# A second PSUM bank for the first MLP's pre-activations, its stores on SP's queue, and a later start for the first block's attention pairs

## The chip, the cores and the metric

The kernel runs on one core of a Trainium2 chip. The core has five engines that matter here: TensorE (PE, matrix products; its weight loads are listed apart as PEld), VectorE (DVE), ScalarE (ACT), GpSimd (POOL) and SyncE (SP, which here only issues DMAs). PE writes its results to PSUM, of which the kernel uses 8 banks of 128 partitions x 512 fp32 values. The metric is device time in microseconds (us); lower is better.

## The reference

Three stages follow each other. Cut to what matters:

```python
# attention: B, H, S, D = 4, 8, 576, 64; causal window of 128
scores = scale * q @ k.T
scores = where((rel >= 0) & (rel < 128), scores - slopes * abs(rel), -1e9)
attn = exp(scores - max) / (sum + 1e-9)
x = (attn @ v) as 2304 tokens x 512
# first MLP, 512 -> 2048 -> 512
h = x @ w_in;  g = where(h > 0, h, exp(min(h, 0)) - 1);  x = g @ w_out
# second MLP, 512 -> 2048 -> 512
h = x @ w_in2; g = maximum(0.01 * h, h);                 out = g @ w_out2
```

## The kernel before

**Precision.** Every MLP product is split in three matmuls (`split_mm`, L244): each fp32 operand is held as a rounded value and a remainder. The weights come raw from HBM and are split on chip, in 16 pieces per layer (`w_a1`, `w_a2`, `w_ts`, `w_add`, `w_hi`, `w_lo`; L161 to L196): for each piece two ACT passes (L169, L174), a shift and two adds on DVE, one more ACT pass (`w<-wraw`), and a subtraction on POOL and on DVE. `w_tick` (L223) does one such step.

**Attention.** It is done in 36 pairs of steps (a block of 256 tokens and two heads each). A pair goes through `scores` (S: matmuls into PSUM banks s0 and s1, minimum on DVE, exponentials on ACT, normalization on POOL), then `transposes` (T: PE, copied out by ACT as `pt`, masked by `selects` on POOL), then `values` (V: matmuls into `av_ps`). V's result is taken out by a cast on ACT (`values_cast`) and a subtraction on DVE (`values_rest`), which write the first MLP's input `x1`.

**Order of the work.** The first 8 pairs run ahead of everything, in a loop over `FIRST` = 16 steps, in an order written by hand (`Ordered.on`); weight pieces 0 to 2 are converted in it, at the places that `EARLY` gives. Then the first MLP runs over `BLK1`, token blocks J of 512, 256, 512, 512 and 512. A block has 16 tasks c, one per weight piece: `mlp1_h` (12 matmuls into `h_ps`; then exp on ACT L516, two DVE passes L517 and L518, a cast on ACT L519, a subtraction L521 on POOL and DVE) and, two tasks later (`Y_LAG`), `mlp1_y` (12 matmuls that accumulate in banks y0 to y3). The remaining pairs of attention are put between the tasks at the places `starts`. In `first_late` (called inside the first task of J = 0) the last values of the first 8 pairs are computed. Then `mlp2` does the second MLP.

**PSUM banks.** `h_ps` always uses bank "h" (but for one task in "y1", and a few of the last block in "s0"), so the next task's matmuls wait until L518 has read the bank. The transposes of a pair's even step use "h" too; those of its odd step use "s1", as one half of the scores does. `av_ps` uses "c".

**Stores.** When a block's y is complete, `ys` copies go to three buffers (tag "eg", shared with the activations `g`), by ACT and DVE in turn, and are stored to DRAM (`x2T`, L546) by ACT's DMA queue.

A scheduler of the framework places ACT, DVE, POOL and SP instructions outside the hand-written part; PE keeps the program's order.

Of the kernel before, what the change touches and what calls it, by code (L numbers as in the profile page):

```python
# [25 lines left out]
NC = DFF // P  # L26
# [4 lines left out]
BLK1 = [(0, 512), (512, 256), (768, 512), (1280, 512), (1792, 512)]  # L31
# [7 lines left out]

EARLY = [(2, "a1", 0), (3, "a2", 0), (3, "ts", 0), (4, "add", 0), (5, "hi", 0), (6, "lo", 0),  # L40
         (6, "a1", 1), (7, "a2", 1), (7, "ts", 1), (8, "add", 1), (9, "hi", 1), (10, "lo", 1),
         (10, "a1", 2), (11, "a2", 2), (11, "ts", 2), (12, "add", 2), (13, "hi", 2), (14, "lo", 2)]
RAW = 2
RAW_SLOTS = [8, 9, 10, 11, 12, 13, 14, 15]
FIRST = 16
# [38 lines left out]
def attention_elu_leaky_kernel(  # L84
# [11 lines left out]
    nc = tc.nc  # L96
# [34 lines left out]
    x2T = dram.tile([P, NK, NT], F32, name="x2T")  # L131
# [10 lines left out]
    at = {"load": 0, "a": 0, "b": 0, "c": 0}  # L142
# [29 lines left out]
    def w_a2(k):  # L172
        low = raws[k][:, :, :, 0]
        tc.keep_in_program_order(nc.scalar.activation(low, low.bitcast(U32), AF.Copy, scale=2.0 ** -29))  # L174
# [23 lines left out]
    def w_first(k):  # L198
        w_a1(k)
        w_a2(k)  # L200

    def w_second(k):
        w_ts(k)
        w_add(k)

    def w_third(k):
        w_hi(k)
        w_lo(k)
# [14 lines left out]
    def w_tick(last):  # L223

        while at["load"] < min(last, max(at["c"] + STAGED[at["load"] >= NC], W1_EARLY)):
            w_load()
        a, b, c = at["a"], at["b"], at["c"]
        if a < min(last, at["load"]) and a <= b + 1:
            w_first(a)
            at["a"] += 1  # L230
        if b < a:
            w_second(b)
            at["b"] += 1
        if c < b:
            w_third(c)
            at["c"] += 1
# [134 lines left out]
    def scores(k):  # L371

        if 2 * k >= NS:
            return
        ps = score_mm(2 * k)
        score_mm(2 * k + 1, ps, BLK)
        for s in (2 * k, 2 * k + 1):
            score_min(s)
            score_exp(s)
            score_rec(s)  # L380
            score_norm(s)
# [7 lines left out]
    def transposes(s, tag):  # L389

        if s >= NS:
            return
        st = steps[s]
        t = st["t"]
        ps = psp.tile([P, 512], F32, tag=tag, name="pt_ps")
        pt = ptp.tile([P, 512], F32, tag="pt", name="pt")
        st["pt"], st["parts"] = pt, []
        blocks = []
        for t0, n, before, hh, c in st["reg"]:
            if before == P:  # L400
                blocks.append((P, n, c.start, [(t0, n, hh, t0 - P, P), (t0, n, hh, t0, n)]))
            else:
                if before:
                    blocks.append((before, n, c.start, [(t0, n, hh, t0 - before, before)]))
                blocks.append((n, n, c.start + before, [(t0, n, hh, t0, n)]))
        blocks.sort(key=lambda x: (-x[0], -len(x[3])))
        if 0 < s < FIRST:
            warm(ps[:, :BLK], WARM[1])
        col, groups = 0, {}
        for nk, n, c, parts in blocks:  # L410
            tc.keep_in_program_order(nc.tensor.transpose(ps[:nk, col:col + n], t[:n, c:c + nk], ident[:n, :n]))  # L411
            groups.setdefault((nk, len(parts)), []).append((slice(col, col + n), parts))
            col += n
        for (nk, m), g in groups.items():
            c = slice(g[0][0].start, g[-1][0].stop)

            tc.keep_in_program_order(nc.scalar.copy(pt[:nk, c], ps[:nk, c]))  # L417
        st["groups"], st["col"] = groups, col
# [55 lines left out]
    def values_cast(s):  # L474
        if s < NS and steps[s]["out"]:
            xh, _, av = steps[s]["out"]
            act.copy(xh, av)

    def values_rest(s):
        if s < NS and steps[s]["out"]:  # L480
            xh, xl, av = steps[s]["out"]
            dve.tensor_tensor(xl, av, xh.bitcast(F32), op=ALU.subtract)


    def mlp1_h(J, cs, late_work=lambda: None):

        n = BLK1[J][1]  # L490
        xh, xl = X1[J]

        last = J == len(BLK1) - 1
        tag = "s0" if last and cs[0] < LAG2 and (LAG2 - cs[0]) % 2 else "h"
        if J == 0 and cs[0] == 1:
            tag = "y1"
        ps = psp.tile([P, len(cs), n], F32, tag=tag, name="h_ps")
        ws = [weights(1, c, 0) for c in cs]

        late = NK - 1 if cs[0] == 0 else NK  # L500
        order = [(ci, kk) for ci in range(len(cs)) for kk in range(late)]
        order += [(ci, kk) for ci in range(len(cs)) for kk in range(late, NK)]
        for ci, kk in order:
            wih, wil = ws[ci]
            s = slice(kk * P, (kk + 1) * P)
            if (ci, kk) == (0, late):
                late_work()

            split_mm(ps[:, ci, :], wih[:, s], wil[:, s], xh[:, kk, :n], xl[:, kk, :n],
                     ci == 0 and kk == 0, kk == NK - 1, skip_group_check=True)  # L510

        g, hi, lo = (pool.tile([P, 2 * BLK], dt, tag=t, name=t)
                     for pool, t, dt in ((egp, "eg", F32), (glp, "gh", F32R), (glp, "gl", F32R)))
        ps = ps.rearrange("p c n -> p (c n)")
        m = len(cs) * n
        nc.scalar.activation(g[:, :m], ps, AF.Exp)  # L516
        nc.vector.tensor_scalar(g[:, :m], g[:, :m], 1.0, -1.0, op0=ALU.min, op1=ALU.add)  # L517
        nc.vector.tensor_tensor(g[:, :m], ps, g[:, :m], op=ALU.max)  # L518
        nc.scalar.copy(hi[:, :m], g[:, :m])  # L519
        for half, eng in ((slice(0, m // 2), nc.gpsimd), (slice(m // 2, m), nc.vector)):  # L520
            eng.tensor_tensor(lo[:, half], g[:, half], hi[:, half].bitcast(F32), op=ALU.subtract)  # L521
        return hi, lo
# [3 lines left out]
    def mlp1_y(J, cs, gg):  # L526
        gh, gl = gg
        t0, n = BLK1[J]
        per = 512 // n
        if cs[0] == 0:  # L530
            Y[J] = [psp.tile([P, per, n], F32, tag=f"y{i}", name=f"y{i}") for i in range(NK // per)]
        for ci, i, m in [(ci, i, m) for ci in range(len(cs)) for i in range(3) for m in range(NK)]:
            woh, wol = weights(1, cs[ci], 1)
            w, g = ((woh, gh), (woh, gl), (wol, gh))[i]

            matmul(Y[J][m // per][:, m % per, :], w[:, m * P:(m + 1) * P], g[:, ci * n:ci * n + n],
                             start=cs[ci] == 0 and i == 0 and m % per == 0, stop=cs[ci] == NC - 1 and i == 2,
                             skip_group_check=True)
        if cs[-1] == NC - 1:
            for i, y in enumerate(Y.pop(J)):  # L540
                ys = egp.tile([P, per, n], F32, tag="eg", name="ys")
                if i % 2:
                    nc.vector.tensor_copy(ys, y)
                else:
                    nc.scalar.copy(ys, y)
                nc.scalar.dma_start(out=x2T[:, i * per:i * per + per, t0:t0 + n], in_=ys)  # L546


    for x in LOADS:
# [57 lines left out]
        w_early(n)  # L607
    score_rec(FIRST + 1)
    score_norm(FIRST + 1)
    Ordered.on = False  # L610
    at["a"] = at["b"] = at["c"] = 1 + EARLY[-1][-1]
    w_tick(NC)

    pend, done = [], FIRST // 2

    def first_late():
        values_to(FIRST - 1)
        scores(done + 1)  # L620

    for J in range(len(BLK1) - 1):
        t0, n = BLK1[J + 1]
        todo = NPAIR * (t0 + n) // BLK - done
        starts = [i * NC // todo + (NC // todo - 2) // 2 for i in range(todo)]
        for c in range(NC):
            if c in starts:
                head = done == FIRST // 2

                transposes(2 * done + 1, "c" if head else "s1")  # L630
                values_to(2 * done - 1)
                transposes(2 * done, "y0" if head else "h")
                for i in (1, 0):
                    selects(2 * done + i)
                if not head:
                    scores(done + 1)
                done += 1
            elif c == 0 and J:
                values_to(2 * done - 1)
            g = mlp1_h(J, [c], first_late if c == 0 and J == 0 else lambda: None)  # L640
            if len(pend) == Y_LAG:
                mlp1_y(*pend.pop(0))
            if at["c"] < NC:
                w_tick(NC)
            pend.append((J, [c], g))
# [90 lines left out]
    J = len(BLK1) - 1  # L736
# [9 lines left out]
    for x in pend:  # L746
        mlp1_y(*x)
# [50 lines left out]
```

## Time and profile before

| | |
|---|---|
| median of 3 runs | 963.45 us (961.48 to 963.78) |
| the profiled execution | 965.38 us, of which 963.4 us are the span of the profile |
| PE busy | 935.9 us, 97% of the span |
| DVE, ACT, POOL busy | 411.2, 406.5, 236.0 us (43%, 42%, 24%) |
| mean granted clock of PE | 0.989 |
| chain that ended last | 83% PE; DVE 3%, ACT 2% |

PE is the engine that ends last nearly everywhere. A matmul counts as busy for as long as it takes, at a lowered clock too, so the busy time alone doesn't show what PE loses.

### The profile page before, as it was taken

How to read it: one execution, taken by the hardware profiler on the slowest of the kernel's cores; microseconds unless marked ns; L12 is line 12 of the kernel's file. 1: busy time of each engine (PE TensorE's matmuls, PEld its weight loads, DVE VectorE, ACT ScalarE, POOL GpSimd, SP SyncE). 2: the span in 40 equal slices, each digit the busy share in tenths (PEclk: the TensorE clock that was granted, in tenths of full speed). 3: DMA queues.
4: the chain of work that ended last, by engine and by line, in shares of the span. 5: the costliest groups of instructions: out<-in, count | busy, mean ns of one | idle time of the engine just before them, and what ended most of it. 6: DMA issues, size and time to landing. Idle time of an engine off the chain costs nothing.

```text
span 963.4 us, 13126 instructions
## 1 busy us (share of the span) xinstructions
PE 935.9 (97%) x4885; PEld 755.9 (78%) x4885; DVE 411.2 (43%) x1003; ACT 406.5 (42%) x918; POOL 236.0 (24%) x393
## 2 busy tenths in 40 slices
PE   8888999989999999999999999999999999999998
PEld 4566778788777777777878888888888888888886
DVE  5788883455444443444357666421211121111111
ACT  6887763344434343333256666432322232222222
POOL 4864542333343332334123333100000000000000
PEclk9999999899999999999999999999999999999999
DMA  8940420221211011110333335110110010001001
GB/s 279 363 159 23 153 66 22 88 67 53 58 45 45 21 42 64 45 31 1 110 131 133 131 131 179 40 66 1 36 51 1 1 44 1 0 1 44 1 1 44
DMA packets 41758, 66.76 MB, mean 69 GB/s; under 512 B 3680, under 2 KB 27232, under 8 KB 41696
## 3 DMA queue, kind: packets, MB, share of 16 engines
q1 hardware_dynamic: 38704, 61.09, 19.0%
q10 hardware_dynamic: 2992, 4.85, 1.4%
q8 instruction: 38, 0.62, 0.3%
q14 instruction: 24, 0.20, 0.1%
HBM read 56.49 MB, written 9.44 MB: 68 GB/s over the span
## 4 chain that ended last, share of the span: by engine, by line
PE 83%; DVE 3%; ACT 2%; issue 0%; DMA 0%; ACTq 0%; DVEq 0%
PE h_ps L119 38%; PE o_y L119 18%; PE y L119 17%; PE av_ps L119 4%; PE s_ps L119 3%; PE pt_ps L411 2%; PE o_s L119 1%; PE o_c L119 1%; ACT t L110 1%; DVE t L110 1%; DVE eg L518 0%; DVE eg L517 0%; ACT wf L169 0%; ACT wraw L174 0%; DVE stat L110 0%
## 5 line engine op out<-in xcount | busy, mean ns | idle before, releaser
L119 PE MATMUL h_ps<-x,w 128*128 128x512 f32 (+1 forms) x1920 | 429.3, 373 | 10.8 <-DVE eg L518 8.1
L119 PEld LDWEIGHTS h_ps<-x,w 128*128 128x128 f32 x1920 | 337.0, 190 | 83.4 <-DVE eg L518 12.1
L680 DVE TENSOR_TENSOR g2l<-g,g2h 128x512 fp32r<-128x512 f32 (+1 forms) x80 | 52.1, 653 | 269.1 <-ACT g2h L679 269.1
L119 PE MATMUL y<-gh,w 128*128 128x512 f32 (+1 forms) x640 | 159.1, 371 | 2.1 <-DVE eg L518 1.9
L119 PE MATMUL o_y<-w,g2h 128*128 128x512 f32 x512 | 157.7, 389 | 0.0
L675 ACT ACTIVATE g<-h_ps 128x512 f32<-128x512 f32 (+1 forms) x80 | 44.2, 552 | 252.1 <-PE h_ps L119 250.8
L119 PEld LDWEIGHTS y<-gh,w 128*128 128x128 f32 x640 | 114.8, 190 | 23.2 <-DVE eg L518 2.3
L119 PEld LDWEIGHTS o_y<-w,g2h 128*128 128x128 f32 x512 | 96.1, 188 | 20.0
L521 POOL TENSOR_TENSOR gl<-eg,gh 128x256 fp32r<-128x256 f32 (+1 forms) x80 | 71.2, 890 | 161.2 <-ACT gh L519 154.5
L119 PE MATMUL o_y<-w,g2l 128*128 128x512 f32 x256 | 99.6, 389 | 0.0
L110 POOL TENSOR_SCALAR t<-t,stat 128x128 f32<-128x128 f32 (+3 forms) x160 | 63.0, 407 | 90.6 <-DVE stat L110 83.7
L519 ACT CAST gh<-eg 128x512 fp32r<-128x512 f32 (+1 forms) x80 | 46.2, 577 | 89.4 <-DVE eg L518 89.3
L516 ACT ACTIVATE eg<-h_ps 128x512 f32<-128x512 f32 (+1 forms) x80 | 43.9, 551 | 90.7 <-PE h_ps L119 87.8
L110 ACT ACTIVATE t<-t,stat 128x128 f32<-128x128 f32 (+3 forms) x160 | 62.6, 393 | 46.0 <-DVE t L110 32.7
L517 DVE TENSOR_SCALAR eg<-eg 128x512 f32<-128x512 f32 (+1 forms) x80 | 45.5, 569 | 83.3 <-ACT eg L516 81.7
L119 PE MATMUL y<-gl,w 128*128 128x512 f32 (+1 forms) x320 | 79.9, 372 | 0.0
L110 POOL TENSOR_TENSOR w<-wraw,w 128x512 fp32r<-128x512 f32 x32 | 52.7, 1647 | 84.7 <-ACT w L110 84.2
L119 PEld LDWEIGHTS y<-gl,w 128*128 128x128 f32 x320 | 57.9, 192 | 10.2
L110 DVE CUSTOM_DVE_ANT_0 t<-s_ps,bias 128x256 f32<-128x256 f32 (+4 forms) x160 | 51.9, 371 | 16.3 <-PE s_ps L119 15.7
L521 DVE TENSOR_TENSOR gl<-eg,gh 128x256 fp32r<-128x256 f32 (+1 forms) x80 | 42.1, 527 | 38.9 <-ACT gh L519 38.7
L110 POOL TENSOR_SCALAR_AFFINE_SELECT pt<-pt 128x256 f32<-128x256 f32 (+1 forms) x112 | 48.5, 438 | 39.1 <-ACT pt L417 35.2
L119 PEld LDWEIGHTS o_y<-w,g2l 128*128 128x128 f32 x256 | 48.1, 188 | 10.0
(60 smaller groups left out, 788.8 us busy)
## 6 DMA issues: line engine op xcount, KB each, us to landing
wraw<-in_w_in SPq DMA_DIRECT2D x32, 512.0 KB, 3.8
wraw<-in_w_out SPq DMA_DIRECT2D x32, 512.0 KB, 4.7
qkr<-in_kT SPq DMA_DIRECT2D x28, 192.0 KB, 2.9
x2T<-ys ACTq DMA_DIRECT2D x18, 256.0 KB, 2.4
xr<-x2T SPq DMA_DIRECT2D x4, 1024.0 KB, 5.4
qkr<-in_qT SPq DMA_DIRECT2D x28, 128.0 KB, 2.8
out<-os SPq DMA_DIRECT2D x14, 256.0 KB, 2.0
vr<-in_vp SPq DMA_DIRECT2D x16, 192.0 KB, 2.5
```

Of the source, the lines that this page charges most:

```text
L110: ins = f(*args, **kw)
L119: tc.keep_in_program_order(nc.tensor.matmul(*args, **kw))
L411: tc.keep_in_program_order(nc.tensor.transpose(ps[:nk, col:col + n], t[:n, c:c + nk], ident[:n, :n]))
L516: nc.scalar.activation(g[:, :m], ps, AF.Exp)
L517: nc.vector.tensor_scalar(g[:, :m], g[:, :m], 1.0, -1.0, op0=ALU.min, op1=ALU.add)
L519: nc.scalar.copy(hi[:, :m], g[:, :m])
L521: eng.tensor_tensor(lo[:, half], g[:, half], hi[:, half].bitcast(F32), op=ALU.subtract)
L675: nc.scalar.activation(g, ps, AF.Prelu, alpha=0.01)
L680: nc.vector.tensor_tensor(lo, g, hi.bitcast(F32), op=ALU.subtract)
```

## The change

Three things change. (1) In all blocks but the last, `h_ps` alternates between banks "h" and "c": in block 0 the odd tasks use "c", in the others the even ones. "c" is shared with `av_ps`; the use of "y1" goes. (2) The stores of blocks 0 to 2 are issued by SP instead of ACT. (3) In block 0 the pairs start at tasks 3, 7, 11, 15 instead of 1, 5, 9, 13; the scores of pair 9, which stood in `first_late`, move to task 3; weight piece 3 is begun in the hand-written part, and from then on `w_tick` begins piece k + 1 while it ends piece k.

```diff
-         (10, "a1", 2), (11, "a2", 2), (11, "ts", 2), (12, "add", 2), (13, "hi", 2), (14, "lo", 2)]
+         (10, "a1", 2), (11, "a2", 2), (11, "ts", 2), (12, "add", 2), (13, "hi", 2), (14, "lo", 2),
+         (15, "a1", 3)]
...
-        if J == 0 and cs[0] == 1:
-            tag = "y1"
+        if not last and cs[0] % 2 == (J == 0):
+            tag = "c"
...
-                nc.scalar.dma_start(out=x2T[:, i * per:i * per + per, t0:t0 + n], in_=ys)
+                q = nc.sync if J < len(BLK1) - 2 else nc.scalar
+                q.dma_start(out=x2T[:, i * per:i * per + per, t0:t0 + n], in_=ys)
...
-    Ordered.on = False
-    at["a"] = at["b"] = at["c"] = 1 + EARLY[-1][-1]
-    w_tick(NC)
...
     def first_late():
         values_to(FIRST - 1)
-        scores(done + 1)
+        values_cast(FIRST - 1)
+        values_rest(FIRST - 1)
+        w_a2(3)
+        Ordered.on = False
+        at["a"], at["b"], at["c"] = 4, 3, 3
...
-        starts = [i * NC // todo + (NC // todo - 2) // 2 for i in range(todo)]
+        starts = [i * NC // todo + (3 if J == 0 else 0) for i in range(todo)]
...
-                head = done == FIRST // 2
-                transposes(2 * done + 1, "c" if head else "s1")
+                transposes(2 * done + 1, "s1")
                 values_to(2 * done - 1)
-                transposes(2 * done, "y0" if head else "h")
+                transposes(2 * done, "h")
                 for i in (1, 0):
                     selects(2 * done + i)
-                if not head:
-                    scores(done + 1)
+                scores(done + 1)
```

How this moves the instructions is seen at two places. The first is ACT's queue at the start of block 0. `COPY pt<-pt_ps` are the copies of the transposes of pair 8, `eg<-h_ps` is the exponential of a task, `gh<-eg` its cast, and `wf<-wraw`, `wraw<-wraw` and `w_4` are the passes over weight pieces. Before:

```order
L519 CAST gh<-eg 128x512
L169 ACTIVATE wf<-wraw 128x1024
L174 ACTIVATE wraw<-wraw 128x1024
L417 COPY pt<-pt_ps 128x256
L417 COPY pt<-pt_ps 64x256
L417 COPY pt<-pt_ps 128x128
L417 COPY pt<-pt_ps 64x128
L516 ACTIVATE eg<-h_ps 128x512 x2
L110 CAST w_4_917<-wraw 128x2x512
L519 CAST gh<-eg 128x512
```

With the change:

```order
L518 ACTIVATE eg<-h_ps 128x512 x2
L111 CAST w_4_864<-wraw 128x2x512
L521 CAST gh<-eg 128x512
L170 ACTIVATE wf<-wraw 128x1024
L175 ACTIVATE wraw<-wraw 128x1024
L521 CAST gh<-eg 128x512
L170 ACTIVATE wf<-wraw 128x1024
L175 ACTIVATE wraw<-wraw 128x1024
L418 COPY pt<-pt_ps 128x256
L418 COPY pt<-pt_ps 64x256
L418 COPY pt<-pt_ps 128x128
L418 COPY pt<-pt_ps 64x128
```

The four copies stood after the first passes over piece 4; now they stand behind the exponentials of tasks 1 and 2, the end of piece 4 and the first passes over pieces 5 and 6.

The second place is the end of block 0, when its four `ys` are copied and stored. ACT's queue before, with the stores `x2T<-ys`, the cast of V's result (`x_1820`) and the copies of the transposes of the pair at task 2 of block 1:

```order
L545 COPY ys<-y_896 128x512
L545 COPY ys<-y_898 128x512
L546 DMA x2T<-ys 128x512 x3
L110 CAST x_1820<-av_ps 128x256
L546 DMA x2T<-ys 128x512
L417 COPY pt<-pt_ps 128x256 x2
```

ACT's queue there with the change:

```order
L547 COPY ys<-y_843 128x512
L547 COPY ys<-y_845 128x512
L418 COPY pt<-pt_ps 128x256
L111 CAST x_1820<-av_ps 128x256
L418 COPY pt<-pt_ps 128x256
```

And SP's queue with the change, between the loads of queries, keys (`qkr`) and values (`vr`):

```order
L277 DMA qkr<-in_qT 128x256
L278 DMA qkr<-in_kT 128x384
L550 DMA x2T<-ys 128x512 x3
L293 DMA vr<-in_vp 128x3x128
L550 DMA x2T<-ys 128x512
L277 DMA qkr<-in_qT 128x256
```

The four stores have left ACT's queue, so that the first copy of a transpose stands ahead of V's cast and behind no store; on SP they stand between loads, the fourth behind one more load of values.

## Rows read from the trace of the kernel before

**Rows 1.** Busy time by stage: us, PE, PEld, DVE, ACT, POOL, granted clock, DMA share, GB/s.

```profile
47.50:80.20 32.70, 27.63 (x126) 20.89 (x125) 27.75 (x49) 26.29 (x48) 19.53 (x26) 0.95 0.36 125
```

**Rows 2.** Waits over the span: waiter, released by, us in total, times, longest.

```profile
PE h_ps L119 <- DVE eg L518: 8.1, 8, 2.3
PE s_ps L119 <- ACT pt L417: 3.1, 2, 1.9
PEld h_ps L119 <- DVE eg L518: 12.1, 15, 2.8
```

**Rows 3.** Timeline of PE at block 0's start: start, us, what, idle before it.

```profile
49.80 0.66 PE L119 MATMUL av_ps<-pt,qkvr 128*64 128x128 f32 x8
...
62.45 1.44 PE L119 MATMUL y<-gh,w 128*128 128x512 f32 x3 [1.94 <-DVE eg L518]
...
74.65 3.02 PE L119 MATMUL h_ps<-x,w 128*128 128x512 f32 x12 [2.35 <-DVE eg L518]
...
80.23 0.60 PE L411 MATMUL pt_ps<-ident,t 128*128 128x128 f32 x4
```

**Rows 4.** PE in stretches of 2 us: us, busy, granted clock, DMA share, GB/s.

```profile
64.00:66.00 2.00, 2.00 (x6) 0.50 0.00 0
...
174.00:176.00 2.00, 2.00 (x9) 0.50 0.21 59
```

**Rows 5.** Timeline of ACT at the start of block 0.

```profile
48.70 1.11 ACT L169 ACTIVATE wf<-wraw 128x1024 f32<-128x1024 f32 x1
...
66.49 1.15 ACT L169 ACTIVATE wf<-wraw 128x1024 f32<-128x1024 f32 x1
67.53 1.14 ACT L174 ACTIVATE wraw<-wraw 128x1024 int32<-128x1024 uint32 x1
68.56 1.12 ACT L110 CAST w<-wraw 128x1024 fp32r<-128x1024 f32 x1
69.69 0.60 ACT L516 ACTIVATE eg<-h_ps 128x512 f32<-128x512 f32 x1
```

**Rows 6.** Timeline of PE in block 1: where a pair's transposes begin.

```profile
167.99 0.38 PE L411 MATMUL pt_ps<-ident,t 128*128 128x128 f32 x2
...
182.16 0.38 PE L411 MATMUL pt_ps<-ident,t 128*128 128x128 f32 x2
...
228.76 0.38 PE L411 MATMUL pt_ps<-ident,t 128*128 128x128 f32 x2
...
237.29 0.38 PE L411 MATMUL pt_ps<-ident,t 128*128 128x128 f32 x2
```

**Rows 7.** Timeline of DVE, then of ACT with its DMA queue, at block 0's end.

```profile
170.86 0.69 DVE L543 COPY ys<-y 128x512 f32<-128x512 f32 x1 [2.37 <-DMA x2T<-ys]
...
171.59 0.33 ACTq L546 DMA_DIRECT2D x2T<-ys  x1
171.95 0.65 ACT L417 COPY pt<-pt_ps 128x256 f32<-128x256 f32 x2 [1.85 <-DVE x L110]
```

**Rows 8.** Timeline of PE at block 3's start: where transposes begin.

```profile
364.27 0.38 PE L411 MATMUL pt_ps<-ident,t 128*128 128x128 f32 x2
...
382.56 0.38 PE L411 MATMUL pt_ps<-ident,t 128*128 128x128 f32 x2
...
397.49 0.38 PE L411 MATMUL pt_ps<-ident,t 128*128 128x128 f32 x2
```

**Rows 9.** Waits of PE between 190 and 250 us (block 1).

```profile
PE h_ps L119 <- DVE eg L518: 4.3, 5, 0.9
```

**Rows 10.** Timeline of DVE and PE: V's subtraction and the next h.

```profile
112.06 0.42 DVE L110 TENSOR_TENSOR x<-av_ps,x 128x256 fp32r<-128x256 f32 x1
...
111.78 3.02 PE L119 MATMUL h_ps<-x,w 128*128 128x512 f32 x12
...
211.92 0.42 DVE L110 TENSOR_TENSOR x<-av_ps,x 128x256 fp32r<-128x256 f32 x1 [1.04 <-ACT x L110]
...
212.52 1.69 PE L119 MATMUL h_ps<-x,w 128*128 128x256 f32 x12
```

## Prediction

> **What bounds the kernel now.** The chain that ended last is 83% PE, so I looked for the places where PE is held up, first by stage, then by releaser, then in PE's own timeline. In the first 32.7 us of block 0 PE is busy for 27.63 us, while DVE is busy for 27.75 and ACT for 26.29 [rows 1]: this stretch is shared between three engines. Over the whole span PE's matmuls wait 8.1 us for DVE's reading of `h_ps`, and 3.1 us, in two waits, for ACT's copy of transposes, where scores need bank "s1"; weight loads of `h_ps` wait 15 times on the same reading of the bank as matmuls do 8 times [rows 2]. After some of the waits the granted clock is 0.50, the 1.2 GHz level: at 64 to 66 us, behind the wait of 1.94 us, and at 174 to 176 us [rows 3, 4]. So a wait there costs more than its own length, and I price such places by the period of the timeline that holds them.
>
> **Stores by SP (blocks 0 and 2).** At the end of block 0 the fourth `ys` copy on DVE waits 2.37 us for the first store, whose buffer it takes; ACT's queue holds the fourth store until that copy is done, at 171.59; and the transposes' copies stand behind it, with 1.85 us of idle time ahead of them [rows 7]. PE's scores wait for these copies. The pair at 167.99 lasts until the next one at 182.16: 14.17 us. A pair of the same block with no wait, 228.76 to 237.29, lasts 8.53 us [rows 6]. The loss is 5.6 us: the longer wait of the two (1.9 us) [rows 2] and the low clock behind it. In the changed order ACT's first transposes' copy stands behind no store, and V's cast neither. The four stores aren't removed: SP issues them, between loads. It is free there for the first three, and the fourth stands behind a load of values that waits for PE. DVE's fourth copy still waits for the first store and may delay the minimum of the scores by some tenths, but PE needs those only at the next pair. I take the full 5.6 us; at worst, if the minimum's delay goes through, 4.
>
> At the start of block 3 the same chain is there: 364.27 to 382.56 is 18.29 us, the next period, 382.56 to 397.49, is 14.93 [rows 8]. The difference, 3.4 us, goes with it. Block 1 has two stores and no such wait; I count nothing.
>
> A rule speaks against this part. The Trainium skill, DMA: Bandwidth & Descriptors, section "Issuing engines are not separate DMA queues", says that all issuing engines' transfers end up on the same 16 DMA engines and that spreading the issue saves only the sequencer's time, usually small. By that alone the move would be worth the issue times, 0.33 us for the fourth [rows 7], on an engine off the path: about nothing. The trace shows another thing than transfer speed, an instruction queue that is held by a store waiting for another engine; I go by that, and keep the rule's outcome as a rival.
>
> **Two banks for h, block 1.** Between 190 and 250 us PE waits five times for the bank, 4.3 us in all, 0.8 to 0.9 each [rows 9]. It is always the odd task, whose matmuls follow after a single short `y`, while DVE still does the pair's scores before L517 and L518. With the even task in "c", the odd task's bank was emptied by the transposes' copy long before. 4.3 us go. What could take their place is the transposes' own need of normalized scores: all periods fall to about 8.53 us [rows 6], a period that is there already and shows no such need. So the full 4.3; at worst 3.
>
> **Two banks elsewhere.** Weight loads wait 15 times and matmuls 8 times, so some seven tasks lose only a little, a few tenths each where the load is late and the matmul not. I take 0.17 each, 1.2 us in all (between 0 and 2).
>
> **The price of "c".** In 27 pairs (3 in block 0, 24 in blocks 1 to 3) the task after a pair now needs "c" emptied by V's cast and subtraction. Before, it needed the copy of the even transposes. In block 1 the subtraction starts at 211.92 and ends 0.42 later, at 212.34; h starts at 212.52 [rows 10], after the scores. So 0.18 us are left, and it costs nothing while nothing delays DVE. In block 0, where DVE also converts weights, one subtraction runs from 112.06 to 112.48 while h started at 111.78 [rows 10]: there 0.7 us would be lost. Of the three pairs of block 0 I count one such; the small bank waits in block 0 that go (0.2 to 0.4 us each) pay for it.
>
> **The start of block 0.** This is the unclear part. Until the pair at 80.23, PE loses there: 1.94 us and 2.35 us of waits [rows 3] and about half of the 3.5 us at the 1.2 GHz level [rows 4], some 6 us. What the change removes: the scores of pair 9 and the transposes of pair 8 leave the first tasks, so DVE has less ahead of L518, and tasks 1 and 2 no longer wait for one bank. What it adds: at task 3 the transposes go to "s1" and the scores need "s1" again, so PE waits for ACT's copy, which now stands behind two passes over each of pieces 5 and 6. From the ACT rows one pass takes 1.0 us (66.49 to 67.53 to 68.56) and a cast of a piece 1.1 (68.56 to 69.69), an exponential or `gh` about 0.5 [rows 5]. From the first pass of piece 3 at 48.70 [rows 5] up to the copies ACT has eight passes (pieces 3 to 6), two casts of pieces, three exponentials, three `gh` (one per task 0 to 2) and a cast of V: 8.2 + 2.2 + 3.0 + 0.3 = 13.7 us, and four waits for DVE or PE of 0.5 to 0.9 us each, estimated from the chain (each cast of a piece waits for an add on DVE that waits for the pass ahead of it), 2.5 in all. The copies come at about 65. PE meanwhile, from the values at 49.80 to 50.46 on [rows 3], has the last three matmuls of task 0 (0.7 us), three dozens (tasks 1 and 2 and one `y`) of at most 3.0 us each [rows 10] and transposes of 0.6 [rows 3]: it is done at about 61. A wait of some 4 us, with a stretch of low clock behind it, 2 us more: 6 us again. So I take 0 for the start. If ACT's own work alone decided, with no waits in between, the copies would come at 62.5, the wait would be 1.5 us and the gain about 4; if the clock stays low through task 3 and beyond, the loss is about 4.
>
> **Sum.** 5.6 + 3.4 + 4.3 + 1.2 = 14.5 us, the rest zero. The profiled execution took 965.38 us (span 963.4), so its counterpart would take 950.9. The median of the runs, 963.45, is 1.9 below that execution; against it the sum gives 949.0.
>
> **Rivals.** (a) The start of block 0 gains 4 us, since the wait for the copies is short: 945. (b) It loses 4 us, for the wait is long and the clock low: 953. For both speaks that my walk rests on waits that no row shows. (c) "c" binds a little: V's cast and subtraction come 0.3 us later than the scores end in 27 pairs, 8 us: 957. For it speaks the margin of only 0.18 us; against it that the cast stands in ACT's queue right where it stood. (d) The stores by SP bring nothing but issue time, as the rule has it: the 9.0 us stay, 958. Against it speaks that what waits is ACT's queue, for a copy, and not a transfer [rows 7]. (e) The other side: DVE is late for V's subtraction by 0.7 us in every pair, as in the one pair at 112.06 [rows 10], since L517 and L518 of the odd task now come earlier and stand ahead of it: 27 x 0.7 = 18.9, 968. From (14.5 + 2.9) / 27 = 0.64 us per pair on the change is slower; at 0.54 us it makes no difference, 963.5. Against it speaks that DVE is idle for 1.04 us before the subtraction in block 1 [rows 10]. (f) The banks in turn don't remove block 1's wait, for the transposes then wait for normalized scores: the 4.3 us stay, 953.
>
> **Numbers.** 0.3% (2.9 us) is about what a measurement of this kernel can tell from no change. The forecast, 946 to 952, gets 0.60; (a) 0.10, (b) 0.11, (c) 0.07, (d) 0.03, (f) 0.03, (e) 0.03 slower and 0.03 about equal. Faster is all but (e): 0.94, and 0.03 each for the others. The range leaves out the (e) cases, half of (c) and (d) and a part of (a): 943 to 957.
>
> **What would show it.** After: no wait of scores for ACT's copies at the ends of blocks 0 and 2, and no granted clock of 0.5 there; in block 1 no wait of h for L518 and periods of 8.5 us; one wait of scores for ACT's copy at task 3 of block 0, of about 4 us. I am wrong if h waits for V's subtraction in many pairs, if the periods of block 1 don't fall, or if block 0 as a whole moves by more than 4 us.

## The result and the profile after

| | before | with the change |
|---|---|---|
| median | 962.47 us (961.47 to 963.78, 4 runs) | 950.93 us (950.91 to 951.09, 4 runs) |
| ratio | | 0.9879 [0.9865, 0.9893] |
| the profiled execution | 965.38 us, span 963.4 | 951.09 us, span 949.3 |
| its mean granted clock of PE | 0.989 | 0.995 |

The change gains 11.5 us between the medians; forecast were 949.0 us and a range of 943 to 957. The forecast took its 14.5 us from 963.45; from the 962.47 of this table they lead to 948.0. The profiled execution of before, from which the prediction read its prices, lies 2.9 us above the median. Of 42 other runs of that kernel, taken beside the experiments, only two took as long, and their mean granted clocks are 0.991 to 0.996.

The page of the changed kernel, busy time and chain:

```profile
PE 928.4 (98%) x4885; PEld 752.4 (79%) x4885; DVE 409.1 (43%) x1003; ACT 407.0 (43%) x918; POOL 234.1 (25%) x393
...
PE 85%; ACT 1%; DVE 1%; issue 0%; DVEq 0%; ACTq 0%
```

PE's waits over the span (waiter, released by, total, times, longest), against [rows 2]:

```profile
PE s_ps L120 <- ACT pt L418: 4.3, 1, 4.3
...
PE h_ps L120 <- DVE x L111: 1.5, 3, 0.6
...
PE h_ps L120 <- DVE eg L520: 1.3, 1, 1.3
```

Eight waits of h for its bank were 8.1 us; one is left (1.3 us, in the last block of the first MLP, which keeps its bank; it was there before too). The two waits of scores at the ends of blocks 0 and 2 are gone, and a new one of 4.3 us is there. Of the three short waits of h for V's subtraction (`x`) two stand in block 0, at 96.90 and 124.07 us (0.39 and 0.55): that is what bank "c" costs there. The third is at the last pair of all (442.71).

PE's timeline: the start of block 0, then the ends of pairs in blocks 1 and 3, against [rows 3, 6, 8]:

```profile
65.50 2.05 PE L120 MATMUL s_ps<-qkr 64*64 64x192 f32 x10 [4.34 <-ACT pt L418]
67.48 5.43 PE L120 MATMUL h_ps<-x,w 128*128 128x512 f32 x12
...
168.76 0.38 PE L412 MATMUL pt_ps<-ident,t 128*128 128x128 f32 x2
...
177.44 0.38 PE L412 MATMUL pt_ps<-ident,t 128*128 128x128 f32 x2
...
219.52 0.38 PE L412 MATMUL pt_ps<-ident,t 128*128 128x128 f32 x2
...
227.96 0.38 PE L412 MATMUL pt_ps<-ident,t 128*128 128x128 f32 x2
...
353.00 0.38 PE L412 MATMUL pt_ps<-ident,t 128*128 128x128 f32 x2
...
367.90 0.38 PE L412 MATMUL pt_ps<-ident,t 128*128 128x128 f32 x2
```

The pair at the end of block 0 takes 8.68 us (168.76 to 177.44) instead of 14.17, a later one in block 1 8.44, and a pair of block 3 14.90. At task 3 of block 0 the h behind the wait takes 5.43 us, where one at full clock takes 2.9. The clock there (stretch, PE busy, granted clock, DMA share, GB/s):

```profile
62.00:64.00 2.00, 0.00 (x0) 0.62 0.00 0
64.00:66.00 2.00, 0.51 (x4) 0.50 0.00 0
...
72.00:74.00 2.00, 2.00 (x9) 0.82 0.00 0
```

It is at its lower level, 1.2 GHz, to about 72 us. ACT's timeline shows the two passes over a weight piece that stood ahead of the transposes' copies:

```profile
62.74 1.12 ACT L170 ACTIVATE wf<-wraw 128x1024 f32<-128x1024 f32 x1
63.77 1.17 ACT L175 ACTIVATE wraw<-wraw 128x1024 int32<-128x1024 uint32 x1
64.84 0.91 ACT L418 COPY pt<-pt_ps 128x256 f32<-128x256 f32 x4
```

**Where the time went.** The stages of the profiled executions, measured in PE's timeline between the first h, the first transposes of blocks 1, 2 and 3, and the end, in us (the last four columns are kernels of the next section; one execution each):

| | before | change | e1_banks | e2_stores | e6_nopairs | e3_pairs |
|---|---|---|---|---|---|---|
| ahead of block 0 | 47.52 | 46.82 | 47.03 | 46.61 | 47.85 | 47.19 |
| block 0 | 107.67 | 109.14 | 107.14 | 107.13 | 108.46 | 106.42 |
| its end and block 1 | 82.10 | 72.00 | 76.20 | 76.93 | 71.99 | 79.06 |
| block 2 | 112.51 | 110.56 | 110.93 | 112.16 | 110.54 | 112.52 |
| from block 3 on | 613.60 | 610.78 | 612.60 | 610.57 | 611.66 | 611.71 |

10.1 of the 14.1 us between the two profiled executions come from the end of block 0 and block 1, 2.0 from block 2, 2.8 from the rest and 0.7 from ahead of block 0; block 0 itself is 1.5 longer. Block 0 is the same in before, e1, e2, e6 and e7 (108.43 there), and took 107.1 to 108.5 us in their executions, so that the 109.14 of the change are only 0.7 above the longest of these.

### The profile page after: what moved, and what is told of

Its sections match the earlier page's. It is cut to its first block, busy times and chain, and to the rows that moved or that the text cites. A ratio compares the mean times of both kernels' runs of the same rounds, so it can differ in the third digit from the quotient of the medians.

```text
span 949.3 us, 13158 instructions
## 1 busy us (share of the span) xinstructions
PE 928.4 (98%) x4885; PEld 752.4 (79%) x4885; DVE 409.1 (43%) x1003; ACT 407.0 (43%) x918; POOL 234.1 (25%) x393
## 4 chain that ended last, share of the span: by engine, by line
PE 85%; ACT 1%; DVE 1%; issue 0%; DVEq 0%; ACTq 0%
PE h_ps L120 39%; PE o_y L120 18%; PE y L120 18%; PE av_ps L120 4%; PE s_ps L120 3%; PE pt_ps L412 2%; PE o_s L120 1%; PE o_c L120 1%; ACT wf L170 0%; ACT wraw L175 0%; DVE wraw L111 0%; DVE eg L519 0%; DVE w L111 0%; DVE eg L520 0%; ACT w L111 0%
## 5 line engine op out<-in xcount | busy, mean ns | idle before, releaser
L523 POOL TENSOR_TENSOR gl<-eg,gh 128x256 fp32r<-128x256 f32 (+1 forms) x80 | 69.8, 872 | 151.2 <-ACT gh L521 139.8
L523 DVE TENSOR_TENSOR gl<-eg,gh 128x256 fp32r<-128x256 f32 (+1 forms) x80 | 42.1, 526 | 39.4 <-ACT gh L521 39.0
L111 DVE CUSTOM_DVE_ANT_0 t<-s_ps,bias 128x256 f32<-128x256 f32 (+4 forms) x160 | 52.0, 371 | 13.4 <-PE s_ps L120 13.2
L120 PEld LDWEIGHTS o_y<-w,g2l 128*128 128x128 f32 x256 | 48.0, 188 | 10.1
```

The costliest lines, as they stand in the source:

```text
L111: ins = f(*args, **kw)
L120: tc.keep_in_program_order(nc.tensor.matmul(*args, **kw))
```

## The experiments

All kernels compute the whole reference; e5_warm adds work. The first four ran on one chip, against 963.44 us of before there (11 runs); e3, e4, e5 and e8 on one against 963.69 (17 runs); e9, e10 and e11 against 961.52 (7); e12 against 962.70 (7). So ratios are what is compared across these groups.

**e1_banks: the banks of blocks 1 to 3 alone, on the kernel before.**

```diff
+        if J and not last and cs[0] % 2 == 0:
+            tag = "c"
```

> The kernel before with one edit: in blocks 1 to 3 the even tasks put h_ps into bank c; block 0, the stores and the pairs stay. My theory (the odd task of block 1 only waits for its one bank): the five waits of 0.8 to 0.9 us in block 1 go, and some tenths at four tasks of block 2, together about 6 us: 956.5 us. The two stalls behind the stores stay. Rival (the pair's own chain of scores, normalization and transposes sets the pace of block 1): the wait turns up ahead of the transposes, and the time stays within 1.5 us of before, 962.

956.40 us, ratio 0.9929 [0.9916, 0.9943]: 7.0 us, as expected. Between 190 and 250 us PE has no wait left. The two waits of scores are still there.

**e2_stores: the stores by SP alone, on the kernel before.**

```diff
-                nc.scalar.dma_start(out=x2T[...], in_=ys)
+                q = nc.sync if J < len(BLK1) - 2 else nc.scalar
+                q.dma_start(out=x2T[...], in_=ys)
```

> The kernel before with one edit: the stores of blocks 0 to 2 go to SP's queue. My theory (ACT's queue is held by the fourth store, which waits for the fourth copy): both stalls behind the stores go, 5.6 and 3.4 us: 953.5 us. Rival (only the issue time is saved, as for a move between queues that share the same DMA engines): 962, unchanged.

957.22 us, 0.9937 [0.9924, 0.9951]: 6.2 us. No wait of scores for ACT's copies is left, as the mechanism wants, but the gain is smaller than the 9.0 of the prediction. PE's timeline at the end of block 0 there:

```profile
166.54 0.38 PE L411 MATMUL pt_ps<-ident,t 128*128 128x128 f32 x2
...
168.29 1.13 PE L119 MATMUL s_ps<-qkr 64*128 64x256 f32 x8
...
175.53 0.38 PE L411 MATMUL pt_ps<-ident,t 128*128 128x128 f32 x2
```

The scores run through, and the pair takes 8.99 us.

**e7_late4: all stores stay on ACT; only the fourth one of blocks 0 and 2 is issued after the next pair.**

```diff
-                nc.scalar.dma_start(out=x2T[...], in_=ys)
+                st = lambda i=i, ys=ys: nc.scalar.dma_start(out=x2T[...], in_=ys)
+                if J in (0, 2) and i == 3:
+                    late_store.append(st)
+                else:
+                    st()
...
                     scores(done + 1)
+                while late_store:
+                    late_store.pop()()
```

> The kernel before with one edit: the stores stay on ACT's queue, but the fourth one of blocks 0 and 2 is issued behind the next pair's transposes and scores. My theory (what counts is that the store stands ahead of the transposes' copies in ACT's queue, not which queue it is on): nearly the same gain as by SP, 8 to 9 us less what issuing costs on ACT: 954 us. Rival (the gain comes from SP's queue itself, as a second queue): at most 2 us, 961.

958.54 us, 0.9949 [0.9935, 0.9964]: 4.9 us, most of what SP's queue brings, without SP; the 954 of the expectation rested on the price of 9.0 that e2 had not borne out either. ACT's queue and PE's scores at the end of block 0 there:

```profile
170.68 0.37 ACT L417 COPY pt<-pt_ps 128x256 f32<-128x256 f32 x1 [1.12 <-PE av_ps L119]
...
172.50 0.33 ACTq L546 DMA_DIRECT2D x2T<-ys  x1
170.66 1.57 PE L119 MATMUL s_ps<-qkr 64*128 64x256 f32 x8
```

The copies run ahead of the fourth store, and the scores run through. So it is the place of the fourth store in ACT's queue that cost the time. From issue to landing the stores take as long by either queue (us in the last place; before, then the change):

```profile
x2T<-ys ACTq DMA_DIRECT2D x18, 256.0 KB, 2.4
x2T<-ys SPq DMA_DIRECT2D x10, 256.0 KB, 2.6
```

The Trainium skill, DMA: Bandwidth & Descriptors, section "Issuing engines are not separate DMA queues", says that transfers issued by different engines run on the same 16 DMA engines, and that issuing from several saves only the issue time. The landing times agree with the first; by the second alone e2 would have given 962.

**e6_nopairs: banks of blocks 1 to 3 and stores; block 0 as before.**

```diff
+        if J and not last and cs[0] % 2 == 0:
+            tag = "c"
...
-                nc.scalar.dma_start(out=x2T[...], in_=ys)
+                q = nc.sync if J < len(BLK1) - 2 else nc.scalar
+                q.dma_start(out=x2T[...], in_=ys)
```

> The change without its third part: banks in turn in blocks 1 to 3 and the stores by SP, block 0 as before. My theory (the later start of the pairs brings nothing at block 0's start and costs 1.5 us there, 113.5 against 112.0 us): both gains add up, 15 us: 947.5 us, some 1.5 to 3 us faster than the whole change. Rival (the pairs' later start is part of the gain): 953 or more.

950.90 us, 0.9873 [0.9858, 0.9888]: the same as the whole change. The 947.5 of my theory, with 1.5 to 3 us won back at block 0, did not come. The two parts add up (7.0 + 6.2 = 13.2, together 12.5), and the third, with block 0's banks, is worth nothing that these runs can tell beside them. It isn't needed for them either.

**e3_pairs: the later pairs alone (the change, with h's banks and the stores as before).**

```diff
-        if not last and cs[0] % 2 == (J == 0):
-            tag = "c"
+        if J == 0 and cs[0] == 1:
+            tag = "y1"
...
-                q = nc.sync if J < len(BLK1) - 2 else nc.scalar
-                q.dma_start(out=x2T[...], in_=ys)
+                nc.scalar.dma_start(out=x2T[...], in_=ys)
```

> The change's third part alone (later pairs in the first block; h on bank h but for the second task, stores by ACT, as before). My theory: it neither gives nor takes at the start of block 0, so 963.5 against 963.4 of before, up to 2.5 more if the odd tasks of block 0 without a bank of their own wait again; a wait of scores for ACT's copies of some 4 us stands at task 3 and the two waits at the ends of blocks 0 and 2 (about 1.2 to 1.9 each) are back. Rival, that the later pairs are what the other two parts need in order to gain, or that they carry some of the 12.5 us: then 960 or less alone, or over 966.

959.84 us, 0.9976 [0.9957, 0.9994], with the widest spread of all (958.4 to 966.3 in 12 runs). It gains 0.6 to 4.1 us alone (the interval), where I had expected none; the median is that of the rival (960 or less), of which e6 excludes the first half: the other two parts gain without it. Nor was the wait of 4 us at task 3 there. PE stood still earlier, where `y` needs bank "y1", which the second task's h still held. Its profile has the wait at the end of block 0 too, and shows why the stores' price is hard to read from one execution:

```profile
60.06 1.46 PE L120 MATMUL y<-gh,w 128*128 128x512 f32 x3 [2.56 <-DVE eg L519]
...
65.97 1.18 PE L120 MATMUL s_ps<-qkr 64*64 64x192 f32 x10 [0.26 <-ACT pt L418]
...
166.41 0.38 PE L412 MATMUL pt_ps<-ident,t 128*128 128x128 f32 x2
...
170.52 1.13 PE L120 MATMUL s_ps<-qkr 64*128 64x256 f32 x6 [1.66 <-ACT pt L418]
...
177.53 0.38 PE L412 MATMUL pt_ps<-ident,t 128*128 128x128 f32 x2
```

The wait is 1.66 us and the pair 11.12, against 14.17 in the profiled execution of before, whose wait was 1.9; behind the wait of e3 the granted clock is 1.00, there it was 0.50 for three stretches and 0.80 for one. Between the two profiled executions, of before and of e3, 4.6 of 6.5 us lie in this pair (3.05) and in the first one of block 3 (1.6), behind waits that the stores by SP remove anyway. That may be why e3's gain is nothing beside the other parts; one execution each doesn't show it.

**e4_defer: the change, with pair 9's scores behind task 3's h and y.**

```diff
-                scores(done + 1)
+                if J or c != 3:
+                    scores(done + 1)
...
                 mlp1_y(*pend.pop(0))
+            if J == 0 and c == 3:
+                scores(done)
```

> The change, with the scores of pair 9 behind task 3's h and y in block 0 instead of ahead of them, so that PE has 6 us of work while ACT comes to the transposes' copies. My theory: the wait of 4.3 us and the low clock behind it (3.9 us lost) are what the start of block 0 still costs; both go, 951 - 8 = 943, or 945 if a little of the wait stays. Rival, the three engines share this stretch, so that the stall comes back at the next bank (task 4's h, or the exponentials of the deferred scores): 949 to 951.

952.99 us, 0.9886 [0.9871, 0.9902], the ratio of the change (0.9879); the 8 us of my theory did not come. The wait at task 3 is gone, and PE comes to the second pair (task 7) at 85.77 instead of 91.83; there it stands still:

```profile
91.88 0.68 PE L412 MATMUL pt_ps<-ident,t 64*128 64x64 f32 x4 [2.93 <-DVE eg L520]
...
95.07 2.05 PE L120 MATMUL s_ps<-qkr 64*64 64x192 f32 x10 [1.68 <-ACT pt L418]
```

The rival was right in kind: the stall moves on, with its low clock (0.50 from 90 to 100 us), most of it to the second pair, and only 0.90 us to a task's bank ahead of that.

**e8_tick: the change, with the weight step of task 2 behind the pair at task 3.**

```diff
                 done += 1
+                if J == 0 and c == 3:
+                    w_tick(NC)
...
-            if at["c"] < NC:
+            if at["c"] < NC and (J or c != 2):
```

> The change, with the weight step of task 2 of block 0 moved behind the pair at task 3, so that two of ACT's passes over a weight piece (2.1 us) stand behind the transposes' copies instead of ahead. My theory, by which ACT's queue sets the wait: it falls from 4.3 to about 2.2 us, 949, or 947 if the low clock is shorter too. Rival, the wait is set by something else than ACT's passes (DVE's adds, or the copies' own inputs), so it stays at 4 and the time at 951; or the later weight piece delays task 5's y, 951 to 953.

952.74 us, 0.9884 [0.9867, 0.9900], again the ratio of the change, where 949 was expected. The wait at task 3 falls as ACT's queue wants, to 2.26; the rest returns at the second pair:

```profile
63.75 1.18 PE L120 MATMUL s_ps<-qkr 64*64 64x192 f32 x10 [2.26 <-ACT pt L418]
...
90.64 0.45 PE L412 MATMUL pt_ps<-ident,t 64*128 64x64 f32 x4 [0.71 <-DVE eg L520]
...
93.87 2.05 PE L120 MATMUL s_ps<-qkr 64*64 64x192 f32 x10 [2.32 <-ACT pt L418]
```

**e5_warm: the change, with 36 matmuls on the identity into the scores' own bank ahead of pair 9's scores.** They are extra work, and the scores overwrite them.

```diff
-        ps = score_mm(2 * k)
+        ps = None
+        if k == FIRST // 2 + 1:
+            ps = [psp.tile([P, 512], F32, tag=tg, name="s_ps") for tg in ("s0", "s1")]
+            warm(ps[0][:, :BLK], 36)
+        ps = score_mm(2 * k, ps)
```

> The change with 36 extra matmuls (128 x 256, on the identity, bf16) into the scores' own bank s0 ahead of pair 9's scores, which overwrite it: added work that falls into the wait for ACT's copies. My theory: the low clock behind the wait comes of PE standing still there; the copies come no later, so that the wait is filled and the clock stays at 1.0: 951 - 3.9 + about 0.5 for what the extra matmuls reach beyond the wait = 947.5. Rival, the low clock there doesn't hang on PE standing still (it is at 0.62 already at 62 to 64): 951 or, with the added work on the path, up to 954.

951.08 us, 0.9867 [0.9852, 0.9882]: nothing gained that is clear of noise. The clock did stay up where the wait was filled, and fell at the second pair, behind waits of 0.19 and 0.66 us there:

```profile
64.00:66.00 2.00, 2.00 (x20) 1.00 0.00 0
...
96.00:98.00 2.00, 2.00 (x6) 0.58 1.07 346
```

Three ways to shorten the start thus came to the same second pair, where V's subtraction on DVE started at 96.50 (e4), 95.25 (e8), 95.45 (e5) and 96.43 (change). Counted from each execution's first h, that is at most 2.3 us earlier than in the change, where wait and low clock at task 3 were 8. So DVE and ACT, more than PE, set the time of block 0 up to there. The change's DVE and POOL in one task of that stretch:

```profile
86.07 1.83 POOL L111 TENSOR_TENSOR w<-wraw,w 128x512 fp32r<-128x512 f32 x1 [3.15 <-ACT w L111]
86.68 1.50 DVE L523 TENSOR_TENSOR gl<-eg,gh 128x256 fp32r<-128x256 f32 x1
87.86 0.92 POOL L523 TENSOR_TENSOR gl<-eg,gh 128x256 fp32r<-128x256 f32 x1
88.11 1.23 DVE L111 TENSOR_SCALAR wf<-wf 128x1024 int32<-128x1024 int32 x1
```

DVE repeats every 5.8 us (L520 at 85.30 and at 91.06 us) with hardly a gap, where a task takes PE 5.44. Its `gl` ends shortly after POOL's subtraction, and takes 0.42 us where it starts just ahead of POOL's half (102.78 us, POOL's at 102.83); its shift ends after POOL's `gl`, and takes 0.69 at 103.81, when POOL's `gl` is done. The Trainium skill, SBUF — State Buffer, section "SBUF: two separate sides", says that DVE and GpSimd share a pair of ports as an exclusive lock for a whole instruction; these rows agree. Hence the next runs.

**e9_sub: the change, with both halves of the subtraction of pieces 3 to 15 on DVE.**

```diff
-            eng = dve if io == 1 else pool
+            eng = dve if io == 1 or 3 <= k < NC else pool
```

> The change with both halves of the subtraction of weight pieces 3 to 15 on DVE (POOL's half goes there). My theory now: between tasks 4 and 12 of block 0 DVE runs back to back at 5.85 us for a task against PE's 5.44, because its L523 (1.5 us, 0.42 where POOL stands still) and its shift (1.23, 0.69) wait for POOL's halves; with POOL's half on DVE (0.69 more) a task costs DVE 5.0 to 5.4, V's subtraction at the second and third pair is no longer late (the three waits of 0.5 of h for it go), and the time falls by 1 to 2, to 949 or 950. Rival, DVE's added 0.69 is simply added (6.5 a task), and PE waits longer for V's subtraction: 955 or more. Or neither matters, as PE is the bound of block 0: 951.

949.06 us, 0.9871 [0.9853, 0.9888]. DVE's groups between 82 and 92 us, first of the change, then of e9 (busy, mean ns, idle before):

```profile
L523 DVE TENSOR_TENSOR gl<-eg,gh 128x256 fp32r<-128x256 f32 x2 | 2.9, 1432 | 0.1
L111 DVE TENSOR_SCALAR wf<-wf 128x1024 int32<-128x1024 int32 x2 | 2.5, 1228 | 0.0
...
L111 DVE TENSOR_TENSOR w<-wraw,w 128x512 fp32r<-128x512 f32 x2 | 1.4, 692 | 0.2
```

```profile
L111 DVE TENSOR_TENSOR w<-wraw,w 128x512 fp32r<-128x512 f32 x4 | 2.6, 686 | 0.1
...
L523 DVE TENSOR_TENSOR gl<-eg,gh 128x256 fp32r<-128x256 f32 x2 | 1.9, 959 | 0.0
...
L111 DVE TENSOR_SCALAR wf<-wf 128x1024 int32<-128x1024 int32 x2 | 1.4, 681 | 0.0
```

DVE does twice the subtractions, and these three kinds together take 5.9 us for two tasks instead of 6.8. The waits of h for V's subtraction in block 0 are gone, and the block takes 106.41 us instead of 109.14; some 1.2 of these 2.7 are a shorter stretch of low clock (2.4 us lost to it behind the wait, against 3.6). The rival's 955 is excluded. Against the change the ratios' intervals overlap.

**e10_sub_defer and e11_sub_tick: e9 with e4's and with e8's edit.**

```diff
-            eng = dve if io == 1 else pool
+            eng = dve if io == 1 or 3 <= k < NC else pool
...
-                scores(done + 1)
+                if J or c != 3:
+                    scores(done + 1)
...
+            if J == 0 and c == 3:
+                scores(done)
```

> Both, POOL's half on DVE and pair 9's scores behind task 3's h and y. My theory, by which what is won at task 3 was given back at the second pair since DVE could not follow: now it is kept, at least in part: 944 to 947. Rival, what is won at task 3 is given back for another reason (ACT's queue ahead of the copies at the second pair): 950 to 953, as without POOL's half on DVE (952.99).

948.29 us, 0.9867 [0.9849, 0.9884]: a little slower than my theory's range. PE still waits at the second pair, 1.0 us for DVE and 2.3 for ACT's copies.

```diff
-            eng = dve if io == 1 else pool
+            eng = dve if io == 1 or 3 <= k < NC else pool
...
+                if J == 0 and c == 3:
+                    w_tick(NC)
...
-            if at["c"] < NC:
+            if at["c"] < NC and (J or c != 2):
```

> Both, POOL's half on DVE and task 2's weight step behind the pair at task 3. My theory: as for the deferred scores, with some 2 us won at task 3 and kept: 946 to 948. Rival: 950 to 953, as without POOL's half on DVE (952.74).

947.22 us, 0.9855 [0.9832, 0.9878], the lowest of all; block 0 takes 105.26 us, and no wait is left at the second pair, as expected. Its interval overlaps that of the change, so that it isn't shown to beat it.

**e12_all: e9's and e8's edits, pair 9's scores behind task 3's h, and L523 of tasks 3 to 12 on DVE alone.** Cut to what is new in it:

```diff
+        if J == 0 and 2 < cs[0] < 13:
+            halves = ((slice(0, m), nc.vector),)
...
+            if J == 0 and c == 3:
+                scores(done)
+                w_tick(NC)
```

> POOL's half of the weights' subtraction on DVE, task 2's weight step behind the pair at task 3, pair 9's scores behind task 3's h alone, and L523 of tasks 3 to 12 of block 0 wholly on DVE as well (0.69 instead of 0.97 beside POOL's half). My theory: DVE needs 5.05 us for a task there, less than PE's 5.44; the wait of 2.0 at task 3 and the low clock behind it (3.4 lost) go, and of these 5.4 us DVE lets 1.5 to 3 be kept: 944 to 946. Rival, DVE's work as a whole up to the second pair is the bound of this stretch, so that nothing more can be had from the order: 947 or more.

949.79 us, 0.9865 [0.9839, 0.9891]: the rival's time, though the longer wait is for ACT and not for DVE. PE has no wait at task 3, comes to the second pair at 83.86 us, and waits there for both:

```profile
88.03 0.69 PE L412 MATMUL pt_ps<-ident,t 64*128 64x64 f32 x4 [0.97 <-DVE eg L520]
...
91.22 2.05 PE L120 MATMUL s_ps<-qkr 64*64 64x192 f32 x10 [1.69 <-ACT pt L418]
```

ACT's timeline has the copy which the scores need behind the two passes over a weight piece again:

```profile
88.75 1.14 ACT L170 ACTIVATE wf<-wraw 128x1024 f32<-128x1024 f32 x1
89.79 1.13 ACT L175 ACTIVATE wraw<-wraw 128x1024 int32<-128x1024 uint32 x1
90.82 0.35 ACT L418 COPY pt<-pt_ps 64x256 f32<-64x256 f32 x1
```

## Why the prediction was right, point by point

**Stores (5.6 + 3.4 = 9.0 forecast).** The mechanism was right: e2 removes both waits, and e7 shows that the place in ACT's queue is the cause. The size was too large: 6.2 us alone, and 5.5 on top of the banks (956.40 to 950.90). The step that failed is "The loss is 5.6 us: the longer wait of the two (1.9 us) and the low clock behind it", and with it the 3.4 of block 3, both read from one execution. The pair with the wait took 14.17 us in before [rows 6], 12.88 in e1 and 11.12 in e3, each with a wait of 1.7 to 2.0; without a wait it takes 8.68 to 8.99. In block 3 the period fell by 3.4 in before [rows 8], and by 1.75 in e1 (16.69 to 14.94) at the same wait of 1.2. The part that differs is the low clock, which didn't follow each wait. In e3's execution, with no low clock at either place, the two cost 2.1 (11.12 against 8.99) and 1.75: 3.9 us, less than the 5.5 to 6.2 of the medians, while the 9.0 have a low clock behind both.

**Banks (4.3 + 1.2 = 5.5 forecast).** 7.0 us alone, 6.3 on top of the stores (957.22 to 950.90). The mechanism was right, the size too small. Only four of the five waits of [rows 9], 3.45 us, stand in block 1; the fifth, at 245.16, is in block 2. Block 1 gains 4.9 (e2 to the change: 76.9 to 72.0), and block 2 1.6. The term was priced by the waits alone, though the prediction means to price by periods. One period of block 1, before (to 228.76 [rows 6]) and with the change (to 219.52):

```profile
219.45 0.38 PE L411 MATMUL pt_ps<-ident,t 128*128 128x128 f32 x2
...
211.28 0.38 PE L412 MATMUL pt_ps<-ident,t 128*128 128x128 f32 x2
```

It fell from 9.31 to 8.24 us, 1.07 for a wait of 0.82; the four periods with a wait fell by 4.45 together. Some 0.1 of it is the h behind a wait, which took 1.70 us and takes 1.60 now. The periods in block 1 are 8.2 to 8.7 us, and no wait for normalized scores came, so (f) is out. The error here is of the other sign than that of the stores and made up for a part of it, which is luck: 14.5 forecast, 12.5 measured with both (e6), 11.5 for the change against its own runs of before.

**Bank "c" (zero forecast).** Two waits of h for V's subtraction in block 0, 0.94 us together, and none in the 24 pairs of blocks 1 to 3 but for the very last (0.55, where before waited 0.46 for ACT's copy). Rivals (c) and (e) are out: DVE is late where it also converts weights.

**The start of block 0 (zero forecast).** The walk through ACT's queue gave copies at about 65, PE done at about 61 and a wait of some 4 us; measured were 64.84, 61.2 and 4.34. The low clock behind it was put at 2 us, and is 3.6 from 65.5 us on (the sum of each stretch's length times what its clock lacks to 1). Block 0 is 1.5 us longer than before in the profiles, yet e6, which leaves block 0 alone, takes as long as the change; so neither (a) nor (b) came. What I did not have is that DVE and ACT, which convert the weights, set when the second pair can go on, so that most of what is won at task 3 is lost there again (e4, e5, e8). That this also held the zero against the kernel before, whose second pair stands two tasks earlier, isn't shown. Nor is any kernel here the change without block 0's bank "c" alone; e3, which lacks it, had the shorter block 0 (106.42 against 109.14).

**Stores as issue time only, (d).** Out by e2.

## What to carry to other kernels

A store that waits for a buffer or a copy holds all that stands behind it in the issuing engine's queue; put it on a queue whose next work isn't on the path, or later. Before removing a wait, find which engine sets the next meeting point: where another engine runs back to back up to there, the wait only moves. And price a wait by its own length plus a range for the clock behind it, from more than one execution.

## What the runs showed of the hardware

The lower clock doesn't follow every wait of the same length: at the end of block 0 waits of 1.94 (before), 2.01 (e1) and 1.66 us (e3) were followed by 3.4, 1.7 and 0 us lost to it, and in block 3 the wait of 1.2 us by 1.7 in before and by nothing in e1. The granted clock (the third number from the end) behind the wait at the end of block 0, first of e1, then of e3:

```profile
172.00:174.00 2.00, 2.00 (x9) 0.53 0.14 43
174.00:176.00 2.00, 2.00 (x13) 0.62 0.50 156
...
172.00:174.00 2.00, 2.00 (x19) 1.00 0.52 152
```

What decides it these runs don't show. DVE's 128x256 subtraction took 1.50 us where a POOL subtraction was already running, and 0.42 where it began 0.05 us ahead of POOL's. So work given to POOL made the engine that it was to relieve slower: two subtractions moved onto DVE (e9), and DVE's subtractions and shifts of two tasks took 0.9 us less, though they were two more.
